# Spare matmuls in TensorE's waits, and one load in place of two, in a one-core decode kernel

## The chip, the cores and the metric

The kernel runs on one core of one Trainium2 chip. The metric is the time of one execution in microseconds (us), measured on the device. Each comparison was run on one chip, with the kernel before beside it in the same rounds. The span of a profile runs from the first to the last instruction that it shows; the time is a little longer, 1.3 to 2.7 us in most runs.

## The reference

One token goes through attention over a cache and a gated layer. The cut version:

```python
# x: 1 x 512; k_cache, v_cache: 8 heads x 65536 x 128; all bf16
q = layernorm(x) @ wq                      # 32 query heads of 128
k, v = repeat(k_cache, 4), repeat(v_cache, 4)
o = softmax(q @ k.T * 128**-0.5) @ v
h = x + o @ wo
g, u = layernorm(h) @ w_gate, layernorm(h) @ w_up      # 512 x 1792 each
out = h + (sigmoid(g) * u) @ w_down
```

Almost all bytes are the two caches, 8 x 33.55 MB. Each is read once and used for a single token.

## The kernel before

SP issues all large loads on one queue, in the order in which the data is used, each as soon as its part of a ring buffer is free. DVE transposes K, PE makes the scores, ACT and DVE the softmax, and PE multiplies by V. PE's program is a loop over heads, and in it over four "parts". A part makes scores for one head and may multiply V of the head before, in "rounds" of 8 matmuls. Only the first part (10 rounds) and the fourth (6 rounds) have rounds:

```python
label("values", "part")
e.reg_mov(m, PARTS[0])
away("br_eq", w, w0, "values0", lambda: section("V0"), "sums")    # first part
e.br_ne(w, w0 - 12, on_true="next", on_false="values3")           # second and third: no rounds
label("values3")
...
section("V3")
goto("sums", "values")
...
section("B")                                   # one round: 8 matmuls
e.reg_alu(p, p, s, ALU.add)
... # three more register steps
e.br_ne(m, 0, on_true="sums", on_false="sums_end")
label("sums_end")
away("br_eq", w, w0 - 12, "outs", lambda: section("O"))           # output of a head
```

The end of the program is a chain: the last two rounds of the last V piece, the output of the last head, layer norm, gate and up matmuls, the product, a transpose, 56 down matmuls, copies, store. The loads for it come last in the queue:

```python
W_SPLIT = {"wg": [(0, 4)], "wu": [(0, 3), (3, 4)]}     # w_up in two transfers
WD_SPLIT = [(0, 8), (8, 12), (12, 14)]                 # w_down in three
```

## Time and profile before

| | before |
|---|---|
| time, median of 3 runs | 658.21 us (658.20 to 658.58) |
| span of the profile | 656.0 us |
| bytes read | 282.33 MB, 430 GB/s over the span |
| mean granted clock of TensorE | 0.770 |

The first section of the page has each engine's busy time, with its share of the span and its number of instructions; the first line of the fourth has the chain that ended last, by engine.

```profile
PE 439.9 (67%) x2315; PEld 70.0 (11%) x1547; DVE 350.2 (53%) x432; ACT 42.8 (7%) x114; POOL 3.6 (1%) x17
...
PE 2%; DVE 0%; issue 0%; ACT 0%
```

The profiled run took 657.36 us, 0.9 us less than the median: its tail is one of the shortest. The 22 runs of this kernel beside the experiments have spans of 656.0 to 657.4 us.

PE looks like the busiest engine, and the chain names PE first. But the chain adds up to 2% or so of the span: it was followed back only from the end to 636 us, so it tells nothing of the 636 us before.

### The profile page before, as it was taken

The page shows a single profiled execution, that of the slowest core. Times are in us where ns is not written, and L with a number is a line of the kernel's source. Part 1 is how long each engine was busy: PE and PEld are TensorE (multiplying, and loading weights), DVE is VectorE, ACT ScalarE, POOL GpSimd, SP SyncE. Part 2 cuts the span into 40 slices and gives each one's busy share as a digit, 9 for nine tenths or more (in the row PEclk, how much of TensorE's full clock was granted, in tenths as well). Part 3 has the DMA queues.
Part 4 walks back from the last instruction along what each step waited for, and adds up shares of the span by engine and source line. Part 5 has one row for each costly group of instructions (what it writes and reads, how often), then busy time and mean ns, then how long its engine had stood idle before and what let it go on. Part 6 is the DMA issues. An engine that isn't in the chain of part 4 may idle for free. (4 is left out here: it accounts for less than half of the span.)

```text
span 656.0 us, 6289 instructions
## 1 busy us (share of the span) xinstructions
PE 439.9 (67%) x2315; PEld 70.0 (11%) x1547; DVE 350.2 (53%) x432; ACT 42.8 (7%) x114; POOL 3.6 (1%) x17
## 2 busy tenths in 40 slices
PE   0698577837678567766677467694767766765765
PEld 0200010101001010010100100010100101001222
DVE  2299846847266645637258380684536572573102
ACT  1100200020000200011000200002000020002001
POOL 1000000000000000000000000000000000000000
PEclk9979788768778577786597786776777956877677
DMA  9999999999999999999999999999999999999998
GB/s 400 432 448 432 432 416 435 432 447 430 448 432 432 432 418 439 447 441 429 418 448 432 432 428 444 444 444 432 402 446 432 432 432 432 464 432 412 422 431 351
DMA packets 8498, 282.33 MB, mean 430 GB/s; under 512 B 1073, under 2 KB 1074, under 8 KB 1586
## 3 DMA queue, kind: packets, MB, share of 16 engines
q1 hardware_dynamic: 8354, 282.33, 99.6%
q10 hardware_dynamic: 144, 0.00, 0.0%
HBM read 282.33 MB, written 0.00 MB: 430 GB/s over the span
## 5 line engine op out<-in xcount | busy, mean ns | idle before, releaser
L496 DVE STREAM_TRANSPOSE ktw<-ring 128x1024 f32<-128x1024 f32 x256 | 292.3, 1208 | 162.1 <-DMA ring<-in_A_k_cache_dram 162.1
L415 PE MATMUL PS<-ktw 128*128 128x512 bf16 x1024 | 293.5, 439 | 103.1 <-DVE ktw L496 96.7
L415 PE MATMUL PS<-ring,PT_sb 128*32 x1024 | 108.3, 517 | 66.5 <-PEq L171 36.7
L415 PEld LDWEIGHTS PS<-ktw 128*128 x256 | 27.2, 106 | 359.6 <-issue 255.9
L585 ACT ACTIVATE po_sb<-PS,rl 128x512 bf16<-128x512 f32 x8 | 5.5, 687 | 521.5 <-PE PS L415 521.5
L415 PEld LDWEIGHTS PS<-ring,PT_sb 128*32 x1024 | 21.7, 116 | 149.1 <-issue 147.4
L503 DVE TENSOR_REDUCE M_sb<-PS 128x1 f32<-128x512 f32 x32 | 19.9, 683 | 19.9 <-PE PS L415 19.9
L531 DVE TENSOR_REDUCE gmj<-PS 1x4 f32<-1x128 f32 x8 | 2.2, 279 | 44.2 <-PE PS L529 44.2
L542 ACT ACTIVATE P_sb<-PS,negmax 128x512 bf16<-128x512 f32 x32 | 21.5, 685 | 0.3
L552 DVE STREAM_TRANSPOSE PT_sb<-P_sb 128x512 bf16<-128x512 bf16 x32 | 20.1, 682 | 1.7 <-ACT P_sb L542 1.7
L386 PE MATMUL PS<-st,onesf 128*128 128x2 f32 x4 | 1.2, 363 | 17.1 <-DVE st L385 17.1
L601 DVE TENSOR_TENSOR Lw<-O,blk_of 128x896 bf16<-128x896 bf16 (+1 forms) x2 | 1.4, 682 | 19.2 <-ACT O L591 19.2
L415 PE MATMUL PS<-ring,xz 128*8 x32 | 9.0, 452 | 2.3 <-issue 2.3
L529 PE MATMUL PS<-identf,gm 128*1 128x128 f32 x16 | 4.5, 380 | 5.4 <-issue 3.3
L536 PE MATMUL PS<-one_f,gmrep 1*128 1x1 f32 x16 | 4.4, 345 | 5.0 <-DVE gmrep L533 5.0
L559 DVE TENSOR_REDUCE lsum<-PS 128x1 f32<-128x4 f32 x8 | 1.3, 162 | 11.3 <-PE PS L557 11.3
L415 PE MATMUL PS<-ktw,O 128*1 x26 | 7.2, 443 | 0.0
L542 ACT ACTIVATION_READ_ACCUMULATOR P_sb<-PS,negmax 128x1 f32 x32 | 6.5, 203 | 0.0
L401 DVE CAST hT<-x_col 128x4 f32<-128x4 bf16 x1 | 0.2, 170 | 11.7 <-DMA x_col<-in_A_x_dram 11.7
L588 PE MATMUL PS<-sel_bf,po_sb 128*128 128x4 bf16 x32 | 2.1, 171 | 6.3 <-ACT po_sb L585 6.3
L460 DVE STREAM_TRANSPOSE qt<-qh 32x512 bf16<-32x512 bf16 x1 | 0.7, 699 | 10.5 <-ACT qh L457 10.5
L557 PE MATMUL PS<-L_sb,lsel 128*128 128x4 f32 x16 | 2.5, 229 | 3.8 <-DVE PT_sb L552 3.8
(82 smaller groups left out, 69.5 us busy)
## 6 DMA issues: line engine op xcount, KB each, us to landing
ring<-in_A_k_cache_dram SPq DMA_DIRECT2D x16, 6144.0 KB, 24.3
ring<-in_A_v_cache_dram SPq DMA_DIRECT2D x15, 6144.0 KB, 25.7
ring<-in_A_v_cache_dram SPq DMA_DIRECT2D x9, 4096.0 KB, 30.1
ring<-in_A_k_cache_dram SPq DMA_DIRECT2D x8, 4096.0 KB, 24.7
ring<-in_A_wq_dram SPq DMA_DIRECT2D x1, 4096.0 KB, 12.1
ktw<-in_A_wo_dram SPq DMA_DIRECT2D x1, 3584.0 KB, 14.6
ring<-in_A_v_cache_dram SPq DMA_DIRECT2D x1, 2048.0 KB, 38.3
ring<-in_B_w_gate_dram SPq DMA_DIRECT2D x1, 1792.0 KB, 29.6
```

The lines of the kernel that those rows point to most:

```text
L415: return e.add_instruction(mybir.InstMatmult(name=nc.get_next_instruction_name(), engine=mybir.EngineType.PE, ins=[rhs, lhsT], outs=[e.low ...
L496: op("dve", lambda e, d=dst, sr=src: e.transpose(d, sr), deps, f"T{b}.{c}", to="T")
L503: op("dve", lambda e, u=u: e.tensor_reduce(M_sb[:, u % 4:u % 4 + 1], ps(u % NS, 0, 512), AX.X, ALU.max), [f"S{b}.{NC - NR + k}"], f"mx{u}" ...
L529: op("pe", lambda e: e.matmul(ps(MISC, 0, 128, 0, 1), lhsT=gm[:, :], rhs=identf[:, :], start=True, stop=True), [f"gm{h}"], f"gmT{h}", to="Q")
L531: op("dve", lambda e: e.tensor_reduce(gmj[:, :], ps(MISC, 0, 128, 0, 1).rearrange("p (i a c) -> p a i c", a=4, c=NC), AX.XY, ALU.max), [f" ...
L536: op("pe", lambda e: e.matmul(ps(MISC, 128, 129), lhsT=gmrep[0:1, :], rhs=one_f[0:1, 0:1], start=True, stop=True), [f"gmrep{h}"], f"neg{h}")
L542: op("act", lambda e, b=b: e.activation(P_sb[:, (b % 4) * 512:(b % 4 + 1) * 512], ps(b % NS, 0, 512), AF.Exp, bias=negmax[:, k:k + 1], sca ...
L552: op("dve", lambda e, b=b: e.transpose(PT_sb[:, (b % 4) * 512:(b % 4 + 1) * 512], P_sb[:, (b % 4) * 512:(b % 4 + 1) * 512]), [f"E{b}"], f" ...
L557: op("pe", lambda e: e.matmul(ps(MISC, 132, 136), lhsT=lsel[:, :], rhs=L_sb[:, :], start=True, stop=True), [f"PT{NR * h + NR - 1}"], f"l{h ...
L585: op("act", lambda e: e.activation(po_sb[:, :], ps(PO, 0, 512), AF.Copy, scale=rl[:, :]), [f"PV{h}.{NR - 1}", f"rl{h}"], f"po{h}", to="po")
L588: op("pe", lambda e, t=t: e.matmul(ps(OX, 0, 4), lhsT=po_sb[:, t * 128:(t + 1) * 128], rhs=sel_bf[:, 8 * t:8 * t + 8:2], start=(t == 0), s ...
L601: op("dve", lambda e: e.tensor_tensor(Lw[i][:, :].rearrange("p (j c) -> p j c", j=n), bass.AP(tensor=O2, offset=j0, ap=[[NQ, 128], [1, n], ...
```

## The change

TensorE's granted clock is 0.770 in the mean and falls to 0.50 in some stretches, among them the gate and up matmuls (0.50 from 648 to 651 us, against 1.00 from 652 to 653). The change is meant to keep it up; that filling PE's waits does so was my assumption here, and e1 and e2 test it. Spare matmuls, whose results nobody reads, go into PE's waits, with PSUM bank 5 as their target. Three stand at the head of each part, one after each round, three around the output of a head, and one before the last layer norm. Besides, w_up is loaded in one transfer.

```diff
-        W_SPLIT = {"wg": [(0, 4)], "wu": [(0, 3), (3, 4)]}
+        W_SPLIT = {"wg": [(0, 4)], "wu": [(0, 4)]}
 ...
+        def warm(e, n=1, load=True):
+            for i in range(n):                 # 128 x 504 matmul of qz with ident, into bank 5;
+                ...                            # weights loaded for the first at most
 ...
             e.reg_mov(m, PARTS[0])
+            warm(e, 3)
             away("br_eq", w, w0, "values0", lambda: section("V0"), "sums")
 ...
             section("B")
+            mm_at(e, ps(5, 0, 504, 96, 128), at_reg(PT_sb, reg(e, 11), ...), e.lower_ap(qz[:, 0:504]), True, 32, 96, kept=True)
 ...
-            away("br_eq", w, w0 - 12, "outs", lambda: section("O"))
+            def outs():
+                warm(e, 2)
+                section("O")
+                warm(e, 1, load=False)
+
+            away("br_eq", w, w0 - 12, "outs", outs)
 ...
         project(range(NQ - GS, NQ), O3, ["O3.1", "wo1"], last=True)
+        op("pe", lambda e: warm(e, 1, load=False))
```

More of the change, by code (lines that the diff above doesn't have):

```diff
@@ L418, in mm_at @@
                 bass_skip_group_check=True, **more))
+        def warm(e, n=1, load=True):
+            for i in range(n):
+                more = dict(ldweights=False) if i or not load else {}
+                e.add_instruction(mybir.InstMatmult(
+                    name=nc.get_next_instruction_name(), engine=mybir.EngineType.PE, ins=[e.lower_ap(qz[:, 0:504]), e.lower_ap(ident[:, :])],
+                    outs=[e.lower_ap(ps(5, 0, 504))], start_tensor_calc=True, stop_tensor_calc=True, tile_size=(128, 128),
+                    tile_position=(0, 0), bass_skip_group_check=True, **more))
         regs, R, here = [], {}, OrderedEngineSet([mybir.EngineType.PE])
@@ L716, in pe_flow @@
             section("B")
+            mm_at(e, ps(5, 0, 504, 96, 128), at_reg(PT_sb, reg(e, 11), [[PT_ROW, 128], [4, 32]]), e.lower_ap(qz[:, 0:504]), True, 32, 96, kept=True)
             e.reg_alu(p, p, s, ALU.add)
```

## The prediction

> **What bounds the kernel now.** I read the page's slices first, then its DMA queues, then equal stretches of the steady part, then who waited for whom, then the last microseconds. The slices and the queue part:
>
> ```profile
> PE   0698577837678567766677467694767766765765
> PEclk9979788768778577786597786776777956877677
> DMA  9999999999999999999999999999999999999998
> q1 hardware_dynamic: 8354, 282.33, 99.6%
> ```
>
> DMA is at nine tenths in all slices but the last; one queue carries 282.33 MB and fills its 16 engines for 99.6% of the span. PE is at six or seven tenths, at a granted clock that swings (mean 0.770 by the list of cores). To see whether the stream is at its ceiling, I cut the steady part into five stretches of one head each (77.4 us, the repeat distance of the K and V loads; columns are length, busy time and count of each engine, clock, DMA share, GB/s):
>
> ```profile
> 132.00:209.40 77.40, 52.77 (x266) 7.26 (x170) 42.10 (x50) 4.68 (x13) 0.00 (x0) 0.74 1.00 434
> 209.40:286.80 77.40, 52.55 (x274) 7.21 (x173) 42.75 (x51) 4.68 (x13) 0.00 (x0) 0.76 1.00 434
> 286.80:364.20 77.40, 53.34 (x270) 7.21 (x170) 42.38 (x50) 4.68 (x13) 0.00 (x0) 0.74 1.00 434
> ```
>
> Each head takes the same time at 434 GB/s and share 1.00. A head has 2 x 65536 x 128 x 2 bytes = 33.55 MB, and 33.55 MB / 434 GB/s = 77.3 us: the length of a head is the length of its transfer. PE is busy 53 of 77.4 us, DVE 42. The waits say the same:
>
> ```profile
> DVE ktw L496 <- DMA ring<-in_A_k_cache_dram: 162.1, 20, 16.6
> PE PS L415 <- DVE ktw L496: 96.7, 89, 4.1
> PE PS L415 <- PEq L171: 36.7, 14, 5.3
> ```
>
> DVE waits 162 us for K data, and PE mostly for DVE, which waits for DMA. The queue's own waits name PE and DVE (buffers must come free), but they cost nothing while earlier transfers are still under way. All K and V loads of the cache:
>
> ```profile
> DMA to landing us min/median/max: 17.8/25.7/38.3
> ```
>
> A 4 MB load takes 4.19 MB / 434 = 9.7 us of stream, so even the shortest issue-to-landing time, 17.8 us, has some 8 us of earlier work ahead of it; in the steady heads the least is 24.3 us, against at most 14.5 us for a 6 MB load, so 10 us. **A release may be some 8 to 10 us late before the stream has a hole.**
>
> The end is where a faster PE could count:
>
> ```profile
> 650.00:651.00 1.00, 1.00 (x16) 0.28 (x8) 0.43 (x1) 0.54 (x1) 0.00 (x0) 0.50 1.02 434
> 652.00:653.00 1.00, 0.00 (x0) 0.00 (x0) 0.96 (x2) 0.00 (x0) 0.00 (x0) 1.00 1.01 404
> 653.00:654.00 1.00, 0.95 (x56) 0.76 (x56) 0.00 (x0) 0.00 (x0) 0.00 (x0) 1.00 0.21 80
> ...
> 648.19 3.15 PE L801 MATMUL PS<-ring,hc 128*1 128x448 bf16 x32 [0.25 <-DVE hc L788]
> ...
> 652.35 0.65 DVE L814 STREAM_TRANSPOSE hhT<-hh 128x448 bf16<-128x448 bf16 x1
> 653.04 0.81 PEld L819 LDWEIGHTS PS<-ring,hhT 128*1 128x1 bf16 x56 [1.43 <-DVE hhT L814]
> 653.05 0.99 PE L819 MATMUL PS<-ring,hhT 128*1 128x128 bf16 x56 [1.24 <-DVE hhT L814]
> ```
>
> The stream is full until about 653.3. The chain that ended last runs through compute from 636 us on, and its gate and up matmuls (L801, 3.15 us) run at half clock. But the page's issue list gives the last w_down piece 36.0 us from issue to landing, and the timeline has its issue at 617.66: it lands at 653.7. (Where a consumer waits for a load, it starts at that time: the K load issued at 118.40 takes 24.3 us, and DVE starts on it at 142.72.) The last 8 of the 56 down matmuls need that piece. The other 48, started at 653.05 and some 13.5 ns apart (0.75 us between first and last start, over 55), are through by 653.7. **Both paths meet at 653.7, to within 0.1 us**; after that come 0.3 us of matmuls, 0.6 us of copies, and the store.
>
> [...] the clock column shows 0.50 and 1.00 in short stretches, and in a warm stretch 16 score matmuls take 3.76 us, 235 ns each, against a mean of 293.5 / 1024 = 287 ns. [...]
>
> **The change part by part.** *Spare matmuls.* Three per part of a head that has values (4 parts x 8 heads x 3 = 96), one per round of values (1024 / 8 = 128), three per head around its output (24), one before the last layer norm: 249, with 40 weight loads. [...] The one in each round falls into a gap: rounds show 0.63 us busy and 0.48 us idle[...]. The return is at most 128 scores a head x (287 - 235) ns = 6.7 us[...]. Both lie beside a full DMA stream: on the path, 0 us.
>
> *The end.* Two spares fit into the 0.69 us of the output's ACT copy, one into the 0.6 us before the layer norm's sum. If the clock stays up, L801 goes from 3.15 to some 1.6 us, and small matmuls gain 0.2 us, so the transposed hidden vector is ready at some 651.3 in place of 653.0. But w_down's last piece still lands at 653.7: of 1.7 us, up to 0.1 us reaches the end.
>
> *w_up in one transfer.* Same bytes. The second piece lands at 616.27 + 33.1 = 649.4; the whole will too. At the old clock the up matmuls start half way through L801, at 649.75, so they don't wait; with a warm PE they do, until 649.4, and are still done near 650.2, 2.7 us before the old path needs them. The split costs the engines a little: in the trace's packet records 10752 bytes take 404 ns, 3584 take 140, 14336 take 535. So 9 ns for each of 8 rows per engine, with one semaphore write of 9 ns, are saved: 0.08 us, and this is on the path, as it is in the stream ahead of w_down. SP's 0.43 us of issue goes too, hidden by the 30 us queue.
>
> Sum: 658.2 - 0.08 - 0.05 (half of the up to 0.1) = 658.1 us.
>
> **Rivals.** *A: PE's chain, not the stream, sets the end.* For it: the chain of waits names only compute from 636 us on. Against: the landing at 653.7, and 48 matmuls that end there. If the landing mattered less than I read, 1.7 us come back: 656.5 us, still within 2%. *B: the spares get in the way.* PE gives buffers back later, the stream gets holes, and eight heads pay. For it: SP waits for PE 163 us before cache loads[...]. Against: 8 to 10 us of queued work, and PE idle for 24.6 us a head. It would take another 10 us a head before 1 us is lost; if it did, 8 x 2 to 5 us: 674 to 698 us. *C: the stream moves at another pace* for a warmer PE[...]. Nothing speaks for it: at clock 0.50 and at 1.00 the stretches show the same 420 to 445 GB/s. A change of 0.3% would be 2 us.
>
> **Range and chances.** The runs before spread by 0.4 us, and A and C allow some tenths to each side: 657.3 to 658.9. A change of 13 us needs 2% of a stream that is at 99.6%, so faster is almost excluded, and slower needs B in full: 0.01 faster, 0.98 same, 0.01 slower.
>
> **What would show it.** Right: a head still 77.4 us at 434 GB/s, the queue at 99.6% or a little more; PE's mean clock up from 0.77 to some 0.88, its score matmuls below 439 ns, 249 new matmuls; DVE's wait for K data still over 150 us; the transposed hidden vector 1 to 2 us before 653 and PE's wait ahead of the last down matmuls now ended by the w_down load. Wrong: DMA slices under nine tenths or a least landing time near the 10 to 14 us of bare transfer (B), an end over 1 us earlier after the stream's end (A), a different GB/s in full stretches (C), or a clock that stays at 0.77, which would mean that the spares are too few but would not move the time.

The sum: 658.2 - 0.08 - 0.05 = 658.1 us, in which the spares' cost and their return ("both") counted for 0 us. What a spare costs the trace of the changed kernel shows: three in a row from 633.81 us take 0.80 us at a clock of 1.00, and one alone 0.37, so they start (0.80 - 0.37) / 2 = 0.21 us apart. By that figure, an estimate, the 31 of a head cost 6.5 us; it is also the 0.21 us of the expectations below. One fits between rounds: they start 1.14 us apart with it (444.81 to 445.95) and 1.16 us without it in the kernel before (444.44 to 445.60). That no engine can win anything in the heads rests here on one rate in all of them, 434 GB/s; that this is the most the queue can bring was not shown. (The queue's own waits there, 304 us for DVE and 163 us for PE on cache loads in the whole trace, come with a DMA share of 1.00 in every head.)

## The result, and the profile after

The changed kernel takes 658.39 us in the median of six runs (657.84 to 659.53); the kernel before takes 658.38 us (657.69 to 658.60). The ratio is 1.0003, with a 95% interval of 0.9990 to 1.0015: the same. A ratio is here always the mean time of one kernel's fast runs over that of the other's of the same rounds, so it is not quite the ratio of the medians. (Every experiment below is marked correct; this run has no such mark.)

The slices and the queue of the changed kernel:

```profile
PE   0688587857669567786677676695767966777776
PEclk9989799789889697896887988787978968879798
DMA  9999999999999999999999999999999999999998
q1 hardware_dynamic: 8210, 282.33, 99.6%
```

The clock is higher: its mean is 0.870. The DMA row is what it was, digit for digit, and the queue is filled to the same 99.6%; the single transfer shows as 144 packets fewer. Stretches of one head (length, busy time and count of PE, PEld, DVE, ACT, POOL, then clock, DMA share, GB/s):

```profile
132.00:209.40 77.40, 55.45 (x314) 8.32 (x191) 43.30 (x52) 4.68 (x13) 0.00 (x0) 0.87 1.00 434
209.40:286.80 77.40, 55.60 (x301) 7.75 (x175) 42.20 (x50) 4.68 (x13) 0.00 (x0) 0.85 1.00 434
```

A head still brings its bytes in 77.4 us at 434 GB/s. PE is busy for nearly 3 us more of it, at a clock of 0.85 to 0.87 in place of 0.74 to 0.76. The waits, and the time to landing of all cache loads:

```profile
DVE ktw L504 <- DMA ring<-in_A_k_cache_dram: 150.9, 20, 15.5
PE PS L415 <- DVE ktw L504: 90.2, 83, 4.1
...
PE PS L415 <- PEq L171: 25.0, 13, 2.3
```

```profile
DMA to landing us min/median/max: 17.4/24.9/36.8
```

DVE still waits 151 us for K data. The shortest time to landing fell by 0.4 us, so releases came slightly later, and still with a queue ahead of them. This time the chain could be followed back through the whole span, and it names the transfers first:

```profile
DMA 54%; PE 24%; DVE 13%; issue 8%; ACT 1%; PEld 0%; PEldq 0%; SPq 0%
```

The tail did not go as forecast. These are lines of its timeline in the changed kernel (start, duration, engine, line, operation; in brackets the idle time before):

```profile
633.81 0.80 PE L423 MATMUL PS<-qz,ident 128*128 128x504 bf16 x3 [0.48 <-issue]
...
635.01 0.80 PE L423 MATMUL PS<-qz,ident 128*128 128x504 bf16 x3 [0.41 <-issue]
...
636.16 0.80 PE L423 MATMUL PS<-qz,ident 128*128 128x504 bf16 x3 [0.35 <-issue]
...
637.33 0.63 PE L415 MATMUL PS<-ring,PT_sb 128*32 x8 [0.37 <-issue]
...
648.72 2.79 PE L817 MATMUL PS<-ring,hc 128*1 128x448 bf16 x32 [0.25 <-DVE hc L804]
...
649.51 0.09 PEld L817 LDWEIGHTS PS<-ring,hc 128*1 128x1 bf16 x4 [0.31 <-DMA ring<-in_B_w_up_dram]
...
652.51 0.65 DVE L830 STREAM_TRANSPOSE hhT<-hh 128x448 bf16<-128x448 bf16 x1
...
653.21 0.95 PE L835 MATMUL PS<-ring,hhT 128*1 128x128 bf16 x56 [0.97 <-DVE hhT L830]
```

In the last head, three groups of spares stand between the rounds of the first part and those of the fourth, 1.15 us apart. The first round of the last V piece, which the kernel before started at 636.64, starts at 637.33, though the piece lands at 636.0 in both traces. The gate and up matmuls gain 0.36 us (2.79 against 3.15), and the transposed hidden vector, done at 653.00 before, is done at 653.16. The end of the span moved from 656.0 to 656.1.

### The profile page after: what moved, and what is told of

It reads as the page before. It is cut to its first block, busy times and chain, and to the rows that moved or that the text cites. A ratio compares the mean times of both kernels' runs of the same rounds, so it can differ in the third digit from the quotient of the medians.

```text
span 656.1 us, 6577 instructions
## 1 busy us (share of the span) xinstructions
PE 462.4 (70%) x2564; PEld 73.8 (11%) x1587; DVE 350.3 (53%) x432; ACT 42.9 (7%) x114; POOL 3.6 (1%) x17
## 3 DMA queue, kind: packets, MB, share of 16 engines
q1 hardware_dynamic: 8210, 282.33, 99.6%
## 4 chain that ended last, share of the span: by engine, by line
DMA 54%; PE 24%; DVE 13%; issue 8%; ACT 1%; PEld 0%; PEldq 0%; SPq 0%
DMA ring<-in_A_k_cache_dram 37%; PE PS L415 20%; DMA ring<-in_A_v_cache_dram 15%; DVE ktw L504 11%; DMA x_col<-in_A_x_dram 2%; PE PS L423 2%; ACT P_sb L550 1%; PE PS L817 0%; DVE PT_sb L560 0%; DVE M_sb L511 0%; PE PS L660 0%; PEld PS L415 0%; PEldq L171 0%; PE PS L544 0%; PE PS L386 0%
## 5 line engine op out<-in xcount | busy, mean ns | idle before, releaser
L415 PE MATMUL PS<-ktw 128*128 128x512 bf16 x1024 | 288.6, 432 | 103.5 <-DVE ktw L504 90.2
L415 PE MATMUL PS<-ring,PT_sb 128*32 x1024 | 90.4, 423 | 51.0 <-issue 25.3
L415 PE MATMUL PS<-qz,PT_sb 128*32 128x504 bf16 x128 | 52.9, 413 | 0.0
L415 PEld LDWEIGHTS PS<-ring,PT_sb 128*32 x1024 | 24.9, 116 | 133.0 <-issue 129.2
L423 PE MATMUL PS<-qz,ident 128*128 128x504 bf16 x121 | 33.7, 374 | 2.1 <-issue 2.1
L423 PEld LDWEIGHTS PS<-qz,ident 128*128 128x128 bf16 x40 | 3.8, 96 | 35.2 <-issue 35.2
## 6 DMA issues: line engine op xcount, KB each, us to landing
ring<-in_A_k_cache_dram SPq DMA_DIRECT2D x16, 6144.0 KB, 24.3
```

The costliest lines, as they stand in the source:

```text
L415: return e.add_instruction(mybir.InstMatmult(name=nc.get_next_instruction_name(), engine=mybir.EngineType.PE, ins=[rhs, lhsT], outs=[e.low ...
L423: e.add_instruction(mybir.InstMatmult(name=nc.get_next_instruction_name(), engine=mybir.EngineType.PE, ins=[e.lower_ap(qz[:, 0:504]), e.lo ...
```

## The experiments

The theory was: the stream of loads sets the time of the heads, and in the tail PE's chain and the last load meet, so a faster PE gains nothing. The main rivals were that a chain of compute sets the time, that the spares get in the way, and that the two parts of the change cancel.

### One part of the change at a time

```diff
  e1: the kernel before
-        W_SPLIT = {"wg": [(0, 4)], "wu": [(0, 3), (3, 4)]}
+        W_SPLIT = {"wg": [(0, 4)], "wu": [(0, 4)]}
  e2: the changed kernel
-        W_SPLIT = {"wg": [(0, 4)], "wu": [(0, 4)]}
+        W_SPLIT = {"wg": [(0, 4)], "wu": [(0, 3), (3, 4)]}
```

> The kernel before with w_up in one transfer and no spare matmuls. My theory (the stream of loads sets the time): the same bytes, 128 fewer packets, at most 0.1 us less, so a ratio of 1.000 within the noise of 0.15%, and a mean granted clock of 0.77 as before. Rival (the single transfer makes the up matmuls wait and costs time): 0.3 to 0.5 us more, and PE waiting for w_up in its gate and up matmuls.

> The changed kernel with w_up in two transfers as before. My theory: ratio 1.000 within 0.15%, clock 0.87 as in the changed kernel; each head 77.4 us at 434 GB/s. In the tail the up matmuls need not wait for the whole of w_up. Rival (two parts of the change cancel: the spares gain and the single transfer loses, or the other way): this run and the one with the single transfer alone lie on different sides of 1.000, each by over 0.2%.

Measured: 658.47 us, ratio 1.0005 (0.9989 to 1.0022), and 658.42 us, ratio 1.0001 (0.9984 to 1.0018). Neither part does anything to the time that these rounds can resolve, and they do not lie on two sides of 1.000 by 0.2%. The clocks of the profiled runs are 0.789 and 0.883, so the clock belongs to the spares alone. With w_up in one transfer and the gate and up matmuls as slow as before (3.15 us), no wait for w_up shows in them; the forecast saving of 0.08 us is far below what the runs resolve, and stays unshown.

The profile of e1 shows something else. Its span is 657.1 us, and three of its four runs have 657.1 or more. These are lines of its tail, and of the kernel before:

```profile
642.86 2.16 PE L415 MATMUL PS<-ring,PT_sb 128*32 x16 [1.01 <-issue]
...
654.17 0.95 PE L819 MATMUL PS<-ring,hhT 128*1 128x128 bf16 x56 [1.06 <-DVE hhT L814]
```

```profile
642.14 0.63 PE L415 MATMUL PS<-ring,PT_sb 128*32 x8 [1.00 <-issue]
643.25 0.63 PE L415 MATMUL PS<-ring,PT_sb 128*32 x8 [0.48 <-issue]
```

In e1 the last two rounds took 0.4 us longer than in the kernel before: the second starts at 643.95 and ends at 645.02, and these 1.07 us are about what a round takes there at a granted clock of 0.50 (1.05 us, from 640.08), against 0.63 us for the last two at 1.00. The last piece of w_down landed at 654.4 (issued at 617.97, 36.4 us to landing), and the last 8 down matmuls, counted as in the prediction, came at about 654.8 without a wait. Here PE's chain, not the last load, set the end, by an estimated 0.4 us. The tail is thus not always as even as the one profile before.

### More bytes

```diff
  e3: the kernel before, w_q loaded once more into a free buffer, right behind the first load
+        dma("sp", lambda e: e.dma_start(ktw[:, 0:8 * CH]..., A_wq...), "rx", (), "wqx")
 ...
-                    deps.append(f"S{b - 1}.{c}" if b else None)
+                    deps.append(f"S{b - 1}.{c}" if b else "wqx")
```

> The kernel before with w_q loaded a second time, into a buffer that is free then: 4.19 MB more in the queue, right behind the first load, nothing else changed. My theory (the stream sets the time): 4.19 MB / 434 GB/s = 9.7 us more, so 668.0 us against 658.3, ratio 1.0147. Rival (a chain of compute and waits sets the time, and the full queue is a by-product): well under 9.7 us more, since PE has 24 idle us in each head in which the chain could catch up.

Measured: 668.0 us, ratio 1.0147 (1.0130 to 1.0164). The page's line of packets, here with the 4.19 MB more:

```profile
DMA packets 8642, 286.53 MB, mean 430 GB/s; under 512 B 1089, under 2 KB 1090, under 8 KB 1602
```

The extra bytes cost their full transfer time, to the tenth of a microsecond of the forecast, at the same mean rate. PE's idle time of some 25 us a head absorbed none of it. The extra load stands ahead of the first K load, so it also holds up the chain of compute; but DVE's first transpose starts only 6.9 us later (36.73 us against 29.88), and the time grew by 9.8. The rival, that the full queue is a by-product, falls.

### More spares

```diff
  e4 and e5: the changed kernel, with K = 4 and K = 8
-            mm_at(e, ps(5, 0, 504, 96, 128), at_reg(PT_sb, reg(e, 11), ...
+            for _ in range(K):
+                mm_at(e, ps(5, 0, 504, 96, 128), at_reg(PT_sb, reg(e, 11), ...
```

> The changed kernel with four spare matmuls after each round of values in place of one: 384 more in all, 48 a head. At 0.21 us each that is 10 us a head, of which some 0.27 us of the gap of each of 16 rounds (4 us) absorbs a part. My theory: PE busy grows from 55 to some 64 us a head, still under 77.4, and the time stays, ratio 1.000 to 1.003. Rival (buffers come back late, holes in the stream at once): with 6 us a head on seven heads, over 40 us more, ratio 1.06.

> The changed kernel with eight spares after each round in place of one: 112 more a head, 23.5 us of PE at full clock. My theory: PE then needs some 78 us a head and more where it waits, so it becomes the bound; the stream gets holes, DMA falls under nine tenths, heads grow past 77.4 us: ratio 1.03 to 1.12. If the time still stays at 1.000, PE has far more room than I read. This shows on which side of the slack the change lies.

Measured: 662.42 us, ratio 1.0062 (1.0046 to 1.0079), and 681.86 us, ratio 1.0367 (1.0349 to 1.0384). The sizes are near the expectations (a little over for four), but the place is wrong. Stretches with eight spares, one head and two of the last 80 us:

```profile
209.40:286.80 77.40, 71.02 (x425) 11.48 (x186) 43.67 (x52) 4.68 (x13) 0.00 (x0) 0.96 1.00 434
...
600.00:640.00 40.00, 34.50 (x212) 8.88 (x127) 5.39 (x11) 4.31 (x12) 0.00 (x0) 0.91 0.95 400
...
655.00:660.00 5.00, 5.00 (x43) 1.12 (x22) 0.00 (x0) 0.00 (x0) 0.00 (x0) 1.00 0.10 36
```

And the tail with four (its profiled run took 665.47 us, the slowest of the five):

```profile
650.00:655.00 5.00, 4.28 (x42) 1.41 (x30) 0.72 (x5) 0.86 (x2) 0.00 (x0) 1.00 0.66 269
655.00:660.00 5.00, 2.49 (x36) 1.26 (x36) 2.88 (x12) 0.63 (x1) 0.55 (x1) 1.00 0.00 0
```

I had expected holes in the stream and longer heads. Even with PE busy for 71 of 77.4 us the heads show none: 1.00 and 434 GB/s. The shortest time from issue to landing of a cache load fell from 24.3 us to 17.8 (issues from 130 to 200 us) and 19.8 (200 to 560 us): releases came up to 6.5 us later, inside the 10 us that I had read out of the queue. The loss lies behind these heads. With eight spares the stream ends some 2 us later, after a hole from 605 to 610 us (DMA share 0.57, against 0.85 before). The rest is the tail, where the stream has already ended while PE is still at the last head: PE is busy for all of 655 to 660 us while the DMA share is 0.10. So the heads have room, and the tail has almost none. (Of the 24 us that eight spares cost, some 3.5 are not in the span at all; see the last experiment.)

### Half the bytes

To see what the change does where the stream is not the bound, the K and V loads of heads 2 to 7 bring half their columns; the result is wrong. (The check does not see this error.)

```diff
  e6: the kernel before; e7: the changed kernel
-            a, z = cols or (j0, j1)
+            a, z = cols or ((j0, j1) if h < 2 else ((j0 + j1) // 2, j1))
```

> Wrong result on purpose: the kernel before, where the K and V loads of heads 2 to 7 bring only the second half of their columns (the other half is older data); 97 MB less. The stream alone would end some 225 us earlier, at 433 us. My theory: PE and DVE then set the length of a head, some 58 to 66 us in place of 77.4 with the DMA share near 0.6 to 0.7, so 550 to 600 us. To be read beside the changed kernel with the same halves.

> Wrong result on purpose: the changed kernel with the same halved loads. My theory (the spares do what they are meant to, hidden behind the stream): where the stream does not set the time, the change shows; the spares cost 31 x 0.21 = 6.5 us a head less what the gaps hide, and the clock returns up to 6.7 us a head, so between 2% faster and 3% slower than the halved kernel before. Rival (the spares have no effect at all on PE's work): equal within 0.3%.

Measured: 554.55 us (ratio 0.8418, 0.8398 to 0.8439) and 551.78 us (ratio 0.8381, 0.8367 to 0.8395). The intervals just fail to overlap; 0.8381 / 0.8418 = 0.9956, so the change now gains 0.4%. Stretches of five heads of each, the kernel before first:

```profile
118.00:425.00 307.00, 232.00 (x1332) 35.58 (x850) 212.02 (x248) 23.41 (x65) 0.00 (x0) 0.83 0.77 313
```

```profile
118.00:418.00 300.00, 242.44 (x1486) 37.45 (x875) 211.85 (x248) 23.41 (x65) 0.00 (x0) 0.94 0.79 321
```

From one issue of the same load to the one five heads later it is 118.60 to 425.00 us before, so 61.3 us a head, and 118.56 to 418.08 after, so 59.9. The clock of 0.94 in place of 0.83 is worth 1.4 us a head net of the spares' own cost. In these two profiled runs the changed kernel is 6.7 us ahead when it issues the first load of w_o (496.09 against 502.77) and 4.7 us ahead when it issues the store, so the tail gave 2 us back. The mechanism works and is small. In the real kernel it is hidden behind the transfer of each head.

### The tail

```diff
  e9: the changed kernel, spares only in the parts that have rounds
-            warm(e, 3)
-            away("br_eq", w, w0, "values0", lambda: section("V0"), "sums")
+            def first_values():
+                warm(e, 3)
+                section("V0")
+            away("br_eq", w, w0, "values0", first_values, "sums")
 ...
             e.reg_mov(m, PARTS[3])
+            warm(e, 3)
  e8: e9, and four spares more between the last rounds and the gate matmuls
```

> The changed kernel without spares in the parts that have no rounds (so the last head's rounds start some 0.6 us earlier), and with four more spares in the gaps between the last rounds and the gate matmuls. My theory: the clock stays at 1.0 through the gate and up matmuls, those take some 1.7 us in place of 2.8, the transposed hidden vector is ready at 651 to 652 us, and PE then waits for the last w_down load: the end does not move, ratio 1.000 within 0.15%, span within 0.3 us. Rival (PE's chain in the tail sets the end): an end 1 to 1.5 us earlier after the same last landing.

> The changed kernel with the three spares only in the parts that have rounds of values (first and fourth of each head), so not in the two empty parts; 242 PE instructions in the program against 239. Theory of the tail: in the last head two groups of spares at some 1.15 us each go, so the rounds of the last V piece start at its landing again, some 0.7 us earlier than in the changed kernel, the transposed hidden vector comes some 0.5 us earlier (near 652.6), and the end is the last w_down landing plus 0.3 us of matmuls: span within 0.3 us, ratio 1.000 within 0.15%. Theory of the program's size (see the probe): 242 is still on the near side, so time minus span stays 1.4 to 2.2 us.

Measured: e8 took 661.23 us, ratio 1.0051 (1.0034 to 1.0067), with a span of 656.2 us; e9 took 657.99 us, ratio 0.9996 (0.9979 to 1.0012), with a span of 656.2 us. The spans are as expected in both; the time of e8 is not, and it became the subject of the next experiment. The tail of e9:

```profile
648.22 0.93 PE L821 MATMUL PS<-ring,hc 128*1 128x448 bf16 x16 [0.25 <-DVE hc L808]
...
649.48 0.93 PE L821 MATMUL PS<-ring,hc 128*1 128x448 bf16 x16 [0.33 <-DMA ring<-in_B_w_up_dram]
...
650.40 0.45 DVE L829 TENSOR_SCALAR sg<-sg,rstd 128x448 f32<-128x448 f32 x1 [1.39 <-ACT sg L828]
...
650.97 0.91 DVE L831 TENSOR_TENSOR hh<-PS,sg 128x448 bf16<-128x448 f32 x1
651.91 0.65 DVE L834 STREAM_TRANSPOSE hhT<-hh 128x448 bf16<-128x448 bf16 x1
...
653.81 0.10 PEld L839 LDWEIGHTS PS<-ring,hhT 128*1 128x1 bf16 x8 [0.33 <-DMA ring<-in_B_w_down_dram]
```

Without the spares in the empty parts the chain is 0.6 us earlier than in the changed kernel: the last two rounds start at 642.25 in place of 642.76, and the hidden vector is transposed by 652.56. The gate and up matmuls now run at full clock (1.00), 2 x 0.93 us. In between PE waits for w_up, and before the last 8 down matmuls it waits for w_down. The second wait shows that in this kernel the end is the landing of the last load: PE stands ready, and the span is still 656.2 us. The profiled run of e8 has the same two waits (0.36 us for w_up, 0.20 us for w_down). The rival, an end 1 us or more earlier, falls.

### The time outside the span

The 661.23 us of e8 stand against a span of 656.2, and all four of its runs are 4.8 to 5.1 us over their spans. So are the four runs with eight spares per round. All other kernels up to then are 1.3 to 2.7 us over. What the two have in common is a longer program on PE.

```diff
  e10: the kernel before; after the last down matmul, while the result is copied
+        op("pe", lambda e: tiny(e, 15))      # 15 matmuls of 4 columns into a bank that nobody reads any more
  e11: e8 with warm(e, 1) in place of warm(e, 3) in both parts
  e12: e11 with one spare fewer after the output
-                warm(e, 2, load=False)
+                warm(e, 1, load=False)
```

> The kernel before with fifteen matmuls of 4 columns after its last one, into a bank that nobody reads any more, while the result is copied: 246 PE instructions in the program, as many as in the two runs whose time was 5 us over their span. Theory (the time outside the span depends on the length of PE's program, with a step between 242 and 246): span as before, 656 to 657, but time 661 to 662, ratio 1.005. Rival (those 3.5 us came from what the spares do, not from how many instructions there are): ratio 1.000 and time minus span under 2.2 us.

> The kernel with the dense tail, with one spare in place of three in the parts with rounds: 242 PE instructions. By the theory of the program's size the 3.5 us outside the span vanish again; by the theory of the stream the span stays 656 to 657 with the gate and up matmuls at full clock: ratio 1.000 within 0.15%. Rival (the dense tail itself costs time): ratio 1.005 as with the dense tail.

> The dense tail with one spare per part, less one more spare (after the output's small matmuls one in place of two), so that PE's program has one instruction fewer than the kernel that was 4.8 us over its span. Counted with their weight loads, the spares of the versions written out are: changed kernel 10, four spares per round 13, no spares in empty parts 14, all at 1.3 to 2.5 us over the span; dense tail trimmed 15, probe 16, eight per round 17, dense tail 19, at 3.5 to 5.3 us (one of four runs of the probe at 1.4). Theory (PE's program length, loads counted, with a step between 14 and 15): this one has 14, so time minus span is 1.3 to 1.8 us again, time 658, ratio 1.000. Rival (something else in the dense tail costs those 3.4 us): time minus span stays near 4.8 us, ratio 1.004.

| kernel | spare instructions in PE's program, with weight loads | time less span, us | median time, us |
|---|---|---|---|
| changed kernel | 10 | 1.3 to 2.5 | 658.39 |
| e4, four per round | 13 | 1.3 to 1.7 | 662.42 |
| e9, none in empty parts | 14 | 1.7 | 657.99 |
| e12 | 14 | 1.7 | 657.92 |
| e11 | 15 | 4.8 to 5.0 | 660.97 |
| e10 | 16 | 1.4, 3.6, 3.6, 4.7 | 660.21 |
| e5, eight per round | 17 | 4.8 to 5.1 | 681.86 |
| e8, dense tail | 19 | 4.8 to 5.1 | 661.23 |

(The upper end of the slow group in e12's expectation, 5.3, should read 5.1.) The first form of the theory, a step between 242 and 246 instructions, fell: e11 has 242 by that count, as e4 and e9 have, and is slow (ratio 1.0040, 1.0023 to 1.0057). That count had left out the weight loads. With them counted a step between 14 and 15 fits, and e12 was made to test it. Its whole difference to e11 is one matmul of 0.2 us in a gap, run once a head, and it takes 3.1 us less in the median: ratio 0.9993 (0.9976 to 1.0010). The spans of the two agree within 0.3 us. The probe e10 shows that the extra instructions need not be spares at all, nor stand in the tail's gaps, though one of its four runs lacks the effect and its ratio of 1.0017 (0.9997 to 1.0037) alone would decide nothing. So a step in the time outside the span goes with the length of PE's program. A longer program also moves the code behind it, and no run holds one of the two fixed; by what mechanism the time is lost is open.

e9 and e12 are as good as anything here. On their chip the spans of e9, e11 and e12 are 656.1 to 656.5 us, all below those of the kernel before (656.6 to 657.4). So a chain that comes early takes some 0.6 us off the span. In e9 and e12 part of that is lost outside the span (1.7 us there, 1.3 to 1.6 in the kernel before), and the times, 0.3 to 0.4 us lower in the median, do not separate them from it.

## Why the prediction was right

**The bound.** The stream sets the time: bytes added are paid in full (e3, 9.8 us for 4.19 MB), and a head keeps its 77.4 us with PE busy for 71 of them (e5). Rival C falls as well: 434 GB/s at clocks from 0.74 to 0.96.

**The spares.** The counts were right: 2564 matmuls against 2315, and 40 weight loads more. Rival B was further from coming true than I put it. I had it start to cost when releases come 10 us later; with eight spares per round PE is busy for 17 to 19 us more a head than before, releases come up to 6.5 us later, and no hole comes before the last head. What was mis-sized is the gain. I allowed the score matmuls up to 6.7 us a head; over the kernel their busy time fell from 293.5 to 288.6 us, that is 4.9 us in all and 0.6 us a head. I left out the matmuls with V, whose busy time fell by more, from 108.3 to 90.4 us (part of it may lie in the records alone, which overlap: a spare's lasts 0.37 us with starts 0.21 us apart, and a spare now follows each round). PE's mean clock of 0.87 was forecast as 0.88.

**The tail.** Here the time came out right and the working did not. The step that failed is "so the transposed hidden vector is ready at some 651.3 in place of 653.0": it was ready at 653.16. Three terms were missing or wrong.

- I counted the spares of each part but did not ask where the two parts without rounds stand in the last head. Their spares lie on the chain between two pieces of V, and the first round started 0.7 us later after the same landing. e9 takes two of the three groups away, and the last two rounds start 0.5 us earlier than in the changed kernel.
- I wrote "if the clock stays up". It did not. From 649.5 to 651.5 us the changed kernel's PE is busy for all of 2.00 us at a granted clock of 0.50, so the matmuls took 2.79 us, 0.31 us of waiting for w_up among them, and not 1.6. In e9, with the chain 0.5 us earlier and the same spares around the output, the same matmuls ran at 1.00; no run shows what decides between the two.
- Even at full clock (1.00 in e9; in e8 the same matmuls take the same 2 x 0.93 us) the vector comes at 652.6, since the layer norm's scale, the sigmoid and the product with the scale run beside the up matmuls: in e9 the up matmuls are through near 650.4, but DVE can start the product with them only at 650.97. This second chain was in the timeline of before, hidden under the slow matmuls, and I overlooked it.

The claim that the last landing and PE's chain meet within 0.1 us held in the profiles of the kernel before and of the changed one, where PE was slightly the later (no wait for w_down shows in its tail). It was read from one quick run and does not hold in every run: in e1 PE came some 0.4 us late, and with an earlier chain (e8, e9, e11, e12) PE waits for w_down. That the forecast of 658.1 us still fits owes something to luck, since the chain did not come early at all. Rival A, a gain of 1.7 us, was too large, but partly right: an earlier chain took some 0.6 us off the span (e9, e11, e12), and the tail is the place where PE can cost time, as e4 and e5 show at once.

**The single transfer.** w_up landed at 649.5, against 649.4 forecast, and PE waited for it only where it was fast (0.31 us in the changed kernel, 0.33 in e9). The packet records bear out its working: 128 packets of 10752 bytes (404 ns each) and 128 of 3584 (140 ns) became 128 of 14336 (535 ns), and 16 packets of 4 bytes (9 ns) are gone. In the time the saving of 0.08 us could not be seen.

## What to carry to other kernels

Before you make an engine faster, ask whether the stretch in which it works is as long as its transfer: here one division, bytes of a head by its time, gave 434 GB/s in every head, and adding 4.19 MB, which cost 9.8 us, bore out that the transfer sets the time. A spare instruction that is free in the steady part can stand on the critical chain in the last iteration (here the first round of the last V piece came 0.7 us later), so look at where loop code runs when there is nothing left for it to overlap. Compare span and time for each version: here versions with a longer program cost some 3 us (4.8 to 5.1 us outside the span in e5, e8 and e11, against 1.7 in e9 and e12) that no line of the profile shows.
